# Layer 2 begins with two f pairs of one block, and x forms are written where they are read

## The chip, the cores and the metric

The kernel runs on one core of one Trainium2 chip. The metric is the device time of one execution in microseconds (us), and the figure of a kernel is the median of its runs. PE is the tensor engine, DVE the vector engine, ACT the scalar engine, POOL the GpSimd engine, SP the engine whose queue issues nearly all DMAs.

## The reference

Linear attention over 4 batches, 8 heads, 576 positions, then two feed-forward layers on the 2304 tokens that it yields. All of it is in float32.

```python
x = attn_out.transpose(0, 2, 1, 3).reshape(2304, 512)
def _moe_ref(x, w_in, w_out):      # layer 1: w_in 512 x 2048, w_out 2048 x 512
    h = x @ w_in
    return (h - np.tanh(h)) @ w_out
def _moe2_ref(x, w_in, w_out):     # layer 2, the same shapes
    h = x @ w_in
    return (h * (1.0 / (1.0 + np.exp(-1.702 * h)))) @ w_out
```

## The kernel before

**Splitting.** A float32 operand is written as a high part in float32r and a low part (operand less high part). A product then takes three matmuls (high x high, high x low, low x high). `two` (line 421) makes both parts: a copy on ACT (line 422), then a subtraction on POOL or DVE (line 423).

**Layer 1** (loop at line 720) runs in two halves of 36 steps; step numbers below count within the second half, 0 to 35. A step computes the hidden product of one f tile and one block of 512 tokens (`h_mm`, line 343), the y product of the step three back (`do_y`, line 381) and the nonlinear part (`elem1`): ACT s, w, t; DVE 370; POOL 371; DVE 372 and 373; one step later ACT 355 and POOL 357 split the result. The blocks come in the order 1, 0, 2, 4, 3; block 4 has 256 tokens and takes two f tiles per step. When a block's last y product is done, DVE adds the first half's part into it (`evac`, line 402): the y banks are free for the next block only then. Blocks 0, 1 and 2 end with the y products in steps 18, 10 and 26.

**Work of layer 2 that is done beside layer 1's second half.** From step 4 to 21, `conv_ticks` turns the int64-packed weights of the first three f pairs of layer 2 into Strassen forms: a pair has four raw blocks of 512 KB, and a tick per letter (a, b, s, c and h, d, o and e, one step each). Blocks 0 and 2 lie in a pool of two raw buffers each, 1 and 3 in `raw2`, two buffers; the results go through a ring of four `stg` tiles to DRAM (`wfi`, `wfo`). From step 20, `xprep_ticks` does the same for x of token block 0 (768 tokens; layer 2 has three such blocks): four loads `xi`, then 14 pieces, two per step. A piece makes both parts of one half of one of the seven forms P1 to P7; each of the first eight ends with a difference on DVE (line 532) that a later form needs. A form's half kt 0 has its low part on POOL, kt 1 on DVE. Each piece goes through a ring of four `xo` tiles and a store into DRAM (`xf`); after step 30 the seven forms are loaded back with the weights of pair 0.

Stores are not issued at once: `store` puts them into a list, and `flush(2)` issues those that are two steps old. SP issues its DMAs in program order, and each waits there until its data and its place are ready.

**Layer 2** (loop at line 944) goes through 24 groups (token block sb, f pair j): (0,0), (1,0), (0,1), (1,1) and so on, then block 2 with the pairs in falling order. A group has seven slots. A slot has one Strassen product (six matmuls, `h_prod`, line 816; P2 is computed one group ahead, in slot 5) and one y chunk of an earlier group (six matmuls, line 837; two in slot 3; the first stands in slot 1 of the second group). On DVE a group has sums (`h_add`, 865), products (`mul`, 880) and eight accumulations (845 for the first pair of a block, else 847). `vec` issues them after each slot, ACT and POOL split g (886, 887). The forms of block 1 are made at the start of layer 2 from slot 3 of the first group on (slot count q from 3), those of block 2 from q = 101; both at two pieces per slot. The weights of pair j lie in one of two places, by j mod 2.

```python
GROUPS = [(sb, j) for j in range(NPAIR) for sb in range(2)] + [(2, j) for j in reversed(range(NPAIR))]
SLOTS = ("P1", "P7", "P6", "P4", "P5", "P2", "P3")
...
                if 3 <= q < 98 or q > 100:
                    xticks.popleft()()
                    xticks.popleft()()
```

Of the kernel before, what the change touches and what calls it, by code (L numbers as in the profile page):

```python
# [59 lines left out]
def body(ctx, tc, qT, kT, v, om, w1, w2, out):  # L60
# [20 lines left out]
    xf = dp.tile([7, 128, 4 * TW], F32, name="xf")  # L81
# [343 lines left out]
    def conv_ticks(p, pairs, place=None):  # L425
        raw, st = {}, {}

        def load(q, k):
            if q in pairs:
                o, tag = (cv, ("raw", "ye")[k % 2]) if place or k % 2 == 0 else (p, "raw2")  # L430
                t = raw[q, k] = o.tile([128, 512, 2], I32, tag=tag, name="raw2", bufs=2)
                nc.sync.dma_start(out=t, in_=words(w2[2 * q + k % 2, :, k // 2, :]))
# [31 lines left out]
        def cho(q, k):  # L464
            if place:
                v = place(q)[1][:, k - 2]
            else:
                v = p.tile([128, 2 * 512], F32R, tag="stg", name="stg", bufs=4)
# [6 lines left out]
        def pieces(q):  # L475
# [17 lines left out]
            def out(k):  # L493
                cho(q, k)
                load(q + 1, k)
# [5 lines left out]
        def begin():  # L501
            for k in range(4):
# [4 lines left out]
    def xprep_ticks(sb, tiles, place):  # L507
# [12 lines left out]
        def tick(kt, k):  # L520
# [168 lines left out]
    wpool = {}  # L689

    def new_x2(sb, i):
        t = xform[sb, i] = wpool[sb % 2].tile([128, 2, 2, TW], F32R, tag=f"x{i}", name=f"x{i}", bufs=1)
        return t

    def load_x2(sb, i):
        nc.sync.dma_start(
            out=new_x2(sb, i).bitcast(F32), in_=xf[i].rearrange("p (k h c) -> p k h c", h=2, c=TW))
# [22 lines left out]
    for si, (key, k, fs) in enumerate(steps):  # L720
# [33 lines left out]
        if P and sp >= LAG:  # L754
            flush(2)
# [5 lines left out]
            if sp == 20:  # L761
                xload, xt = xprep_ticks(
                    0, lambda i: rp.tile([128, 2, TW], F32, tag=f"xi{i}", name="xi", bufs=1), None)
# [5 lines left out]
            if sp == 30:  # L769
                flush()  # L770
                assert not ticks and not xticks and not later
                right.close()
                wpool[0] = pool("l2right", side="right", reuse_waits="tile")
                load_x2(0, 0)
                load_win(0)
                for i in range(1, 7):
                    load_x2(0, i)
                load_wout(0)
# [154 lines left out]
    l2 = wpool[1] = pool("l2left", reuse_waits="tile")  # L933
    xload, xt = xprep_ticks(1, lambda i: ya_tile("xi"), lambda i: xform[1, i])
    xload()
    xticks.extend(xt)
# [7 lines left out]
    for n in range(NG + 1):  # L944
        sb, j = GROUPS[min(n, NG - 1)]
        for s in range(7):
# [10 lines left out]
            if n == 0 and s == 1:  # L957
                evac(*ev, 0)
                load_win(1)
                load_wout(1)  # L960
            if n == NG:
                continue
            if s == 0 and n > 2:
                at = GROUPS[n - 1]
                if at[0] == 0 and 1 <= at[1] < NPAIR - 1:
                    (load_wout if at[1] + 1 < NPRE else new_wo)(at[1] + 1)
                elif at[0] == 2 and 0 < at[1] < NPAIR - 1:
                    load_wout(at[1] - 1)
            if s == 0 and n > 1:
                if sb == 0 and 1 <= j < NPAIR - 1:  # L970
                    (load_win if j + 1 < NPRE else new_w)(j + 1)
# [80 lines left out]
```

## Time and profile before

| what | value |
|---|---|
| time, median of 3 runs (lowest to highest) | 932.94 us (932.24 to 934.09) |
| profiled execution: own time, span | 933.93 us, 932.1 us |
| mean granted clock of PE | 0.991 |
| busy: PE, PE weight loads, DVE, ACT, POOL | 906.5, 823.8, 650.5, 564.5, 465.8 us |
| share of the span: PE, PE weight loads, DVE, ACT, POOL | 97%, 88%, 70%, 61%, 50% |
| DMA | 151.83 MB, mean 163 GB/s |

The profile shows one execution. The span runs from its first to its last instruction. The granted clock is the share of full speed (2.4 GHz) that PE was given; 0.5 is 1.2 GHz. In a timeline a row is one instruction or a run of equal ones: start, duration, engine, line, what it writes and reads, and in brackets how long the engine had stood and what ended that. A DMA's landing is counted from its issue.

### The profile page before, as it was taken

The page shows a single profiled execution, that of the slowest core. Times are in us where ns is not written, and L with a number is a line of the kernel's source. Part 1 is how long each engine was busy: PE and PEld are TensorE (multiplying, and loading weights), DVE is VectorE, ACT ScalarE, POOL GpSimd, SP SyncE. Part 2 cuts the span into 40 slices and gives each one's busy share as a digit, 9 for nine tenths or more (in the row PEclk, how much of TensorE's full clock was granted, in tenths as well). Part 3 has the DMA queues.
Part 4 walks back from the last instruction along what each step waited for, and adds up shares of the span by engine and source line. Part 5 has one row for each costly group of instructions (what it writes and reads, how often), then busy time and mean ns, then how long its engine had stood idle before and what let it go on. Part 6 is the DMA issues. An engine that isn't in the chain of part 4 may idle for free.

```text
span 932.1 us, 14425 instructions
## 1 busy us (share of the span) xinstructions
PE 906.5 (97%) x5192; PEld 823.8 (88%) x5192; DVE 650.5 (70%) x1041; ACT 564.5 (61%) x1175; POOL 465.8 (50%) x361
## 2 busy tenths in 40 slices
PE   8999999999999999999979979999999998999998
PEld 6888887888899888888878869999999998999998
DVE  4899978756666655887775374488888888544444
ACT  5888878777777767877647543355555555323231
POOL 3555534546666565776746543235545565222222
PEclk9999999999999999999989998999999999999999
DMA  6787865032453322678755972115443211343532
GB/s 200 231 264 247 257 208 161 23 136 73 131 181 123 127 88 70 223 276 277 256 178 191 410 301 79 46 41 175 170 146 117 88 54 49 124 182 139 234 136 102
DMA packets 56249, 151.83 MB, mean 163 GB/s; under 512 B 6385, under 2 KB 13169, under 8 KB 53873
## 3 DMA queue, kind: packets, MB, share of 16 engines
q1 hardware_dynamic: 56032, 150.57, 47.1%
q8 instruction: 41, 0.67, 0.3%
q10 hardware_dynamic: 144, 0.33, 0.1%
q14 instruction: 32, 0.25, 0.1%
HBM read 104.48 MB, written 46.40 MB: 162 GB/s over the span
## 4 chain that ended last, share of the span: by engine, by line
PE 76%; DVE 12%; POOL 4%; issue 3%; ACT 3%; DMA 1%; SPq 0%; POOLq 0%; ACTq 0%; DVEq 0%
PE hs L837 19%; PE y L816 16%; PE y L381 16%; PE hs L343 15%; PE y L200 3%; DVE xi L532 2%; PE y L183 2%; POOL wq L371 2%; PE y L124 1%; DVE wq L373 1%; DVE raw L294 1%; PE hs L152 1%; DMA wfi<-stg 1%; POOL mq L134 1%; DVE yacc L847 1%
## 5 line engine op out<-in xcount | busy, mean ns | idle before, releaser
L837 PE MATMUL hs<-g,wout 128*128 128x384 f32 x1152 | 226.2, 335 | 0.0
L343 PE MATMUL hs<-xb,w 128*128 128x512 f32 (+1 forms) x960 | 211.1, 370 | 1.5 <-DVE t L372 1.5
L816 PE MATMUL y<-x,win 128*128 128x384 f32 x966 | 196.8, 338 | 7.8 <-ACT x L422 2.9
L837 PEld LDWEIGHTS hs<-g,wout 128*128 128x128 f32 x1152 | 203.0, 189 | 0.0
L381 PE MATMUL y<-ghi,w 128*128 128x512 f32 (+1 forms) x640 | 194.1, 371 | 5.3 <-DVE ye L402 5.2
L343 PEld LDWEIGHTS hs<-xb,w 128*128 128x128 f32 x960 | 168.5, 190 | 32.1 <-DVE t L372 1.7
L887 POOL TENSOR_TENSOR g<-sg,g 128x384 fp32r<-128x384 f32 x96 | 103.3, 1077 | 176.6 <-ACT g L886 173.9
L816 PEld LDWEIGHTS y<-x,win 128*128 128x128 f32 x966 | 170.8, 189 | 11.2 <-DVE hx L865 5.1
L357 POOL TENSOR_TENSOR glo<-wq,ghi 128x512 fp32r<-128x512 f32 x72 | 100.5, 1396 | 139.5 <-ACT ghi L355 139.5
L373 DVE COPY_PREDICATED wq<-m,t 128x512 f32<-128x512 uint16 x72 | 87.6, 1217 | 104.6 <-POOL wq L371 103.5
L847 DVE TENSOR_TENSOR yacc<-hs,yacc 128x384 f32<-128x384 f32 x168 | 92.0, 553 | 84.5 <-PE hs L837 84.5
L381 PEld LDWEIGHTS y<-ghi,w 128*128 128x128 f32 x640 | 118.0, 191 | 26.4 <-issue 6.3
L381 PE MATMUL y<-glo,w 128*128 128x512 f32 (+1 forms) x320 | 118.5, 370 | 0.0
L886 ACT CAST g<-sg 128x384 fp32r<-128x384 f32 x96 | 49.5, 516 | 92.0 <-DVE sg L880 92.0
L877 ACT ACTIVATE sg<-hx 128x384 f32<-128x384 f32 x72 | 37.9, 526 | 109.4 <-DVE hx L865 102.2
L371 POOL TENSOR_TENSOR wq<-wq,s 128x512 f32<-128x512 f32 x70 | 90.6, 1295 | 24.0 <-DVE wq L370 24.0
L134 POOL PARTITION_ALL_REDUCE mq<-pq x32 | 65.9, 2108 | 61.8 <-ACT pq L132 61.8
L363 ACT ACTIVATE s<-hs 128x512 f32<-128x512 f32 x72 | 43.0, 597 | 61.9 <-PE hs L343 61.9
L381 PEld LDWEIGHTS y<-glo,w 128*128 128x128 f32 x320 | 61.1, 191 | 9.9
L355 ACT CAST ghi<-wq 128x512 fp32r<-128x512 f32 x72 | 44.3, 616 | 29.9 <-DVE wq L373 29.9
L370 DVE SCALAR_TENSOR_TENSOR wq<-wq,hs 128x512 f32<-128x512 f32 x72 | 49.0, 681 | 17.7 <-ACT t L365 17.7
L294 DVE SCALAR_TENSOR_TENSOR raw<-raw 128x512 int32<-128x512 int32 x57 | 56.8, 996 | 1.6
(119 smaller groups left out, 1291.4 us busy)
## 6 DMA issues: line engine op xcount, KB each, us to landing
raw<-w SPq DMA_DIRECT2D x57, 512.0 KB, 4.7
xb<-xs SPq DMA_DIRECT2D x24, 512.0 KB, 5.4
win<-wfi SPq DMA_DIRECT2D x9, 1280.0 KB, 8.3
wout<-wfo SPq DMA_DIRECT2D x9, 1024.0 KB, 4.8
xf<-xo SPq DMA_DIRECT2D x14, 384.0 KB, 3.1
x<-xf SPq DMA_DIRECT2D x7, 768.0 KB, 12.5
vt<-v SPq DMA_DIRECT2D x16, 325.0 KB, 3.4
kt<-kT SPq DMA_DIRECT2D x15, 320.0 KB, 3.3
```

Of the source, the lines that this page charges most:

```text
L134: nc.gpsimd.partition_all_reduce(mqs[i, j], pq[:, j, :], channels=128, reduce_op=bass.bass_isa.ReduceOp.max)
L294: nc.vector.scalar_tensor_tensor(out=c, in0=c, scalar=3, in1=z, op0=ALU.logical_shift_left, op1=ALU.bitwise_or)
L343: nc.tensor.matmul(h[:, j * n:j * n + n], w[:, 0, a, kt * 128:kt * 128 + 128], x[:, c, kt, :n], start=(k == 0), stop=(k == 11))
L357: nc.gpsimd.tensor_tensor(out=lo, in0=g, in1=hi.bitcast(F32), op=ALU.subtract)
L371: (nc.vector if si < 2 else nc.gpsimd).tensor_tensor(out=w, in0=w, in1=s, op=ALU.mult)
L373: nc.vector.copy_predicated(out=w, mask=m.bitcast(mybir.dt.uint16), data=t)
L381: nc.tensor.matmul(y[d][:, :n], w[:, 1, a, d * 128:d * 128 + 128], g[c][:, j * n:j * n + n], start=(first and j == 0 and k == 0), stop=(la ...
L816: nc.tensor.matmul(dst, w[:, WID[name], a, kt * 128:kt * 128 + 128], xt[:, kt, c, :], start=(first and k == 0), stop=(k == 5), skip_group_ ...
L837: nc.tensor.matmul(dst, wout[j][:, f, a, d * 128:d * 128 + 128], gt[n, f, t][:, c, :], start=(k == 0), stop=(k == 5))
L847: nc.vector.tensor_tensor(out=u, in0=dst, in1=u, op=ALU.add)
L886: nc.scalar.copy(out=u[:, 0, :], in_=g)
L887: nc.gpsimd.tensor_tensor(out=u[:, 1, :], in0=g, in1=u[:, 0, :].bitcast(F32), op=ALU.subtract)
```

## The change

- `GROUPS` starts with (0,0), (0,1), (1,0), (1,1); from pair 2 on it is as before. So block 1 begins with the third group, and the weights of pairs 0 and 1 are both held until the third and fourth groups; those of pair 2 are loaded one group later.
- The seven forms of block 0 get their place in a pool of their own at the start of the second half of layer 1. The pieces are written there; the ring `xo`, the DRAM tensor `xf`, its 14 stores and 7 loads are gone. That takes room: `raw2` has one buffer for two, `stg` three for four. A pair's block 3 is loaded behind the use of its block 1 (in tick c), the next pair's block 1 behind tick e.
- The pieces for block 0 start at step 24 for step 22, at two and one per step in turn (2, 1, 2, 1, 1 in five steps). Their loads `xi` lie in the room that the weight forms have left, at step 23.
- Layer 2's pieces come one per slot. The weights of pair 1 are asked for ahead of the loads of x.
- Stores are flushed when they are one step old.

The diff, cut to its core:

```diff
-GROUPS = [(sb, j) for j in range(NPAIR) for sb in range(2)] + [(2, j) for j in reversed(range(NPAIR))]
+GROUPS = [(0, 0), (0, 1), (1, 0), (1, 1)]
+GROUPS += [(sb, j) for j in range(2, NPAIR) for sb in range(2)] + [(2, j) for j in reversed(range(NPAIR))]
+XSTEP = 23
...
-                t = raw[q, k] = o.tile([128, 512, 2], I32, tag=tag, name="raw2", bufs=2)
+                t = raw[q, k] = o.tile([128, 512, 2], I32, tag=tag, name="raw2", bufs=1 if tag == "raw2" else 2)
...
-                t = p.tile([128, 2 * 512], F32R, tag="stg", name="stg", bufs=4)[:, :512 * n]
+                t = p.tile([128, 2 * 512], F32R, tag="stg", name="stg", bufs=3)[:, :512 * n]
...
-                load(q + 1, 1)
+                load(*((q + 1, 1) if place else (q, 3)))
...
-                load(q + 1, k)
+                load(q + 1, k if place or k == 2 else 1)
...
-            v = place(i)[:, kt] if place else rp.tile([128, 2, TW], F32R, tag="xo", name="xo", bufs=4)
+            v = xform[sb, i][:, kt]
...
-            if not place:
-                store(xf[i, :, kt * 2 * TW:(kt + 1) * 2 * TW].rearrange("p (a c) -> p a c", c=TW), v.bitcast(F32))
...
         if si == per + LAG - 1:
             wst.close()
+            xpool[0] = pool("x0", side="right", reuse_waits="tile")
+            for i in range(7):
+                new_x2(0, i)
...
-            flush(2)
+            flush(1)
...
-            if sp == 20:
+            if sp == XSTEP:
+                flush()
+                assert not ticks and not later
+                right.close()
+                xr = pool("xprep", right, side="right", reuse_waits="tile")
...
-            elif xticks and sp > 21:
-                xticks.popleft()()
-                xticks.popleft()()
...
+            elif sp > XSTEP and xticks:
+                for _ in range(1 + (sp - XSTEP) % 5 % 2):
+                    xticks.popleft()()
+                if not xticks:
+                    right.close()
+                    wpool[0] = pool("w0", side="right", reuse_waits="tile")
+                    load_win(0)
+                    load_wout(0)
...
+    load_win(1)
...
             if xticks:
                 if 3 <= q < 98 or q > 100:
                     xticks.popleft()()
-                    xticks.popleft()()
-            elif n == 1 and s == 4:
+            elif n == 2 and s == 4:
```

Three places in the order of the instructions. Names: `xi` are the loaded halves of x and its differences, `xo`, `x0` to `x6` forms, `wq` and `t` of `elem1`, `ye` an evacuated block, `hx` and `sg` the sums and products of layer 2. The changed kernel's line numbers are one higher here, three lower in layer 2.

DVE, layer 1, from the predicated copy of step 22 to the evacuation of block 2 in step 26. Before, the rows of steps 24 and 25:

```order
L372 TENSOR_TENSOR t_4800<-hs_4774,t_4800 128x512
L373 COPY_PREDICATED wq_4801<-m_4802,t_4800 128x512
L532 TENSOR_TENSOR xi_4664<-xi_4665,xi_4664 128x384
L423 TENSOR_TENSOR xo_4821<-xi_4668,xo_4821 128x384
L532 TENSOR_TENSOR xi_4668<-xi_4669,xi_4668 128x384
L370 SCALAR_TENSOR_TENSOR wq_4870<-wq_4870,hs_4827 128x512
L372 TENSOR_TENSOR t_4869<-hs_4827,t_4869 128x512
L373 COPY_PREDICATED wq_4870<-m_4871,t_4869 128x512
L532 TENSOR_TENSOR xi_4664<-xi_4665,xi_4663 128x384
L423 TENSOR_TENSOR xo_4890<-xi_4668,xo_4890 128x384
L532 TENSOR_TENSOR xi_4668<-xi_4669,xi_4663 128x384
L370 SCALAR_TENSOR_TENSOR wq_4936<-wq_4936,hs_4897 128x512
```

And now, from the predicated copy of step 24 on:

```order
L374 COPY_PREDICATED wq_4867<-m_4868,t_4866 128x512
L531 TENSOR_TENSOR xi_4813<-xi_4814 128x384
L424 TENSOR_TENSOR x0_3715<-xi_4819,x0_3715 128x384
L531 TENSOR_TENSOR xi_4813<-xi_4818 128x384
L371 SCALAR_TENSOR_TENSOR wq_4929<-wq_4929,hs_4890 128x512
L373 TENSOR_TENSOR t_4928<-hs_4890,t_4928 128x512
L374 COPY_PREDICATED wq_4929<-m_4930,t_4928 128x512
L531 TENSOR_TENSOR xi_4814<-xi_4815,xi_4814 128x384
L403 TENSOR_TENSOR ye_4766<-y0_4428,ye_4766 128x512
L403 TENSOR_TENSOR ye_4766<-y1_4429,ye_4766 128x512
```

Before, three instructions on x stand behind each predicated copy from step 22 to 25, twelve in all ahead of the evacuation; now three behind that of step 24 and one behind that of step 25, and none ahead of them.

SP, layer 1, the middle pair of `conv_ticks` (its first raw loads stand further up). Before, from the load in tick s on:

```order
L432 DMA raw2_4245<-w2 128x1024
L332 DMA xb_4093<-xs_80 128x2x512
L419 DMA wfi_84<-stg_4193 128x1024
L432 DMA raw2_4295<-w2 128x1024
L394 DMA ye_4350<-yp_81 128x2x512
L419 DMA wfi_84<-stg_4292 128x512
L419 DMA wfi_84<-stg_4299 128x1024
L432 DMA raw2_4398<-w2 128x1024
L432 DMA raw2_4403<-w2 128x1024
```

And now:

```order
L433 DMA raw2_4253<-w2 128x1024
L333 DMA xb_4101<-xs_80 128x2x512
L433 DMA raw2_4302<-w2 128x1024
L420 DMA wfi_83<-stg_4299 128x512
L420 DMA wfi_83<-stg_4306 128x1024
L395 DMA ye_4359<-yp_81 128x2x512
L420 DMA wfi_83<-stg_4354 128x1024
L433 DMA raw2_4406<-w2 128x1024
L433 DMA raw2_4411<-w2 128x1024
```

The second raw load of the run was block 1 of the last pair (4295); now it is block 3 of this pair (4302), which tick d reads one step later, and block 1 of the last pair (4411) comes at the end of the run.

DVE, the start of layer 2, from the first product behind the last evacuation on. Before:

```order
L880 TENSOR_TENSOR sg_5607<-hx_5605,sg_5607 128x384
L865 TENSOR_TENSOR hx_5640<-hs_5562,s2_5629 128x384
L532 TENSOR_TENSOR xi_5587<-xi_5588 128x384
L423 TENSOR_TENSOR x0_5596<-xi_5593,x0_5596 128x384
L532 TENSOR_TENSOR xi_5587<-xi_5592 128x384
L865 TENSOR_TENSOR hx_5656<-hs_5543,s7_5609 128x384
L532 TENSOR_TENSOR xi_5588<-xi_5589,xi_5588 128x384
L423 TENSOR_TENSOR x1_5597<-xi_5592,x1_5597 128x384
L532 TENSOR_TENSOR xi_5592<-xi_5593,xi_5592 128x384
L880 TENSOR_TENSOR sg_5654<-hx_5640,sg_5654 128x384
L532 TENSOR_TENSOR xi_5588<-xi_5589,xi_5587 128x384
L423 TENSOR_TENSOR x2_5598<-xi_5592,x2_5598 128x384
```

And now:

```order
L877 TENSOR_TENSOR sg_5583<-hx_5581,sg_5583 128x384
L862 TENSOR_TENSOR hx_5611<-hs_5533,s2_5600 128x384
L531 TENSOR_TENSOR xi_5561<-xi_5562 128x384
L862 TENSOR_TENSOR hx_5624<-hs_5514,s7_5585 128x384
L424 TENSOR_TENSOR x0_5572<-xi_5567,x0_5572 128x384
L531 TENSOR_TENSOR xi_5561<-xi_5566 128x384
L877 TENSOR_TENSOR sg_5622<-hx_5611,sg_5622 128x384
L531 TENSOR_TENSOR xi_5562<-xi_5563,xi_5562 128x384
L877 TENSOR_TENSOR sg_5637<-hx_5624,sg_5637 128x384
L424 TENSOR_TENSOR x1_5573<-xi_5566,x1_5573 128x384
L531 TENSOR_TENSOR xi_5566<-xi_5567,xi_5566 128x384
L862 TENSOR_TENSOR hx_5666<-y1_5659,sp_5639 128x384
```

Before, eight of these twelve make x forms of block 1 (x0 to x2); now six do (x0 and x1), and the sums and products of the first group stand further ahead. From the product that opens the run to the sum that releases P3 of the second group (hx of s7, in slot 4 of that group) there are now 8 differences, 4 low parts, 10 sums and products and 5 copies of y chunks.

## Rows read from the trace of the kernel before

**Rows 1.** PE's waits, 470 us on: total us, times, longest us

```profile
PE y L381 <- DVE ye L402: 5.2, 1, 5.2
```

**Rows 2.** Windows: length, busy PE, PEld, DVE, ACT, POOL, clock, DMA, GB/s

```profile
480.00:490.00 10.00, 8.03 (x43) 7.57 (x44) 5.55 (x8) 0.72 (x3) 2.58 (x3) 0.73 0.68 239
...
560.00:580.00 20.00, 20.00 (x106) 20.00 (x106) 9.84 (x19) 6.74 (x16) 6.61 (x7) 0.90 0.26 93
```

**Rows 3.** Timeline of PE, layer 1: start us, duration us

```profile
432.27 0.47 PE L381 MATMUL y<-ghi,w 128*128 128x512 f32 x1
...
473.70 3.03 PE L343 MATMUL hs<-xb,w 128*128 128x256 f32 x24
...
481.97 0.55 PE L381 MATMUL y<-ghi,w 128*128 128x256 f32 x1 [5.24 <-DVE ye L402]
...
486.46 2.91 PE L343 MATMUL hs<-xb,w 128*128 128x512 f32 x12
...
489.21 0.28 PE L381 MATMUL y<-ghi,w 128*128 128x256 f32 x1
...
492.08 2.91 PE L343 MATMUL hs<-xb,w 128*128 128x512 f32 x12
```

**Rows 4.** Timeline of DVE, layer 1 and (last row) layer 2

```profile
431.44 2.48 DVE L402 TENSOR_TENSOR ye<-y,ye 128x512 f32<-128x512 f32 x4
...
478.68 0.54 DVE L532 TENSOR_TENSOR xi<-xi 128x384 f32<-128x384 f32 x1
...
479.61 1.61 DVE L532 TENSOR_TENSOR xi<-xi 128x384 f32<-128x384 f32 x1
...
481.15 2.47 DVE L402 TENSOR_TENSOR ye<-y,ye 128x512 f32<-128x512 f32 x4
...
550.77 1.36 DVE L532 TENSOR_TENSOR xi<-xi 128x384 f32<-128x384 f32 x1
```

**Rows 5.** Timeline of ACT, layer 1

```profile
408.52 0.67 ACT L283 ACTIVATE raw<-raw 128x512 f32<-128x512 f32 x1
...
414.63 0.62 ACT L355 CAST ghi<-wq 128x512 fp32r<-128x512 f32 x1 [2.17 <-DVE wq L373]
...
469.17 0.51 ACT L422 CAST xo<-xi 128x384 fp32r<-128x384 f32 x1 [0.82 <-DVE xi L532]
...
488.92 0.51 ACT L422 CAST xo<-xi 128x384 fp32r<-128x384 f32 x1 [8.87 <-DMA xf<-xo]
```

**Rows 6.** Timeline of PE, layer 2

```profile
542.28 3.51 PE L816 MATMUL hs<-x,win 128*128 128x384 f32 x18
...
557.98 2.26 PE L816 MATMUL y<-x,win 128*128 128x384 f32 x6 [2.85 <-ACT x L422]
...
568.10 1.20 PE L816 MATMUL y<-x,win 128*128 128x384 f32 x6
...
570.18 1.20 PE L816 MATMUL y<-x,win 128*128 128x384 f32 x6
...
783.59 1.31 PE L816 MATMUL y<-x,win 128*128 128x384 f32 x6 [2.60 <-DVE hx L865]
```

**Rows 7.** Timeline of SP's queue, layer 1

```profile
406.75 0.33 SPq L432 DMA_DIRECT2D raw<-w  x1
...
454.76 2.08 SPq L419 DMA_DIRECT2D wfo<-stg  x2
```

**Rows 8.** Landings: of all raw loads (L432), and of loads issued 436 to 441 us

```profile
DMA to landing us min/median/max: 3.6/5.0/12.0
...
xi<-ysf SPq DMA_DIRECT2D x4, 384.0 KB, 5.5
```

**Rows 9.** Groups of DVE, 543 to 563 us: count, busy us, mean ns

```profile
L532 DVE TENSOR_TENSOR xi<-xi 128x384 f32<-128x384 f32 x8 | 7.7, 960 | 0.0
...
L423 DVE TENSOR_TENSOR x<-xi,x 128x384 fp32r<-128x384 f32 x6 | 5.0, 829 | 0.9 <-ACT x L422 0.9
...
L880 DVE TENSOR_TENSOR sg<-hx,sg 128x384 f32<-128x384 f32 x4 | 2.2, 548 | 0.0
```

More of the change, by code (lines that the diff above doesn't have):

```diff
@@ L467, in cho @@
             else:
[L468 removed]
+                v = p.tile([128, 2 * 512], F32R, tag="stg", name="stg", bufs=3)
                 v = v.rearrange("p (h c) -> p h c", h=2)
@@ L501, in begin, with xprep_ticks @@
         def begin():
-            for k in range(4):
+            for k in range(4 if place else 3):
                 load(pairs[0], k)
         return begin, [(x, f) for q in pairs for x, f in pieces(q).items()]
-    def xprep_ticks(sb, tiles, place):
+    def xprep_ticks(sb, tiles):
         xi = {}
@@ L688, in body @@
     xform, win, wout = {}, {}, {}
-    wpool = {}
+    wpool, xpool = {}, {}
     def new_x2(sb, i):
-        t = xform[sb, i] = wpool[sb % 2].tile([128, 2, 2, TW], F32R, tag=f"x{i}", name=f"x{i}", bufs=1)
+        t = xform[sb, i] = xpool[sb % 2].tile([128, 2, 2, TW], F32R, tag=f"x{i}", name=f"x{i}", bufs=1)
         return t
-    def load_x2(sb, i):
-        nc.sync.dma_start(
-            out=new_x2(sb, i).bitcast(F32), in_=xf[i].rearrange("p (k h c) -> p k h c", h=2, c=TW))
     def new_w(j):
@@ L760, in body @@
                         ticks.popleft()[1]()
-            if sp == 20:
+            if sp == XSTEP:
[3 more added lines that the diff above has]
+                xr = pool("xprep", right, side="right", reuse_waits="tile")
                 xload, xt = xprep_ticks(
-                    0, lambda i: rp.tile([128, 2, TW], F32, tag=f"xi{i}", name="xi", bufs=1), None)
+                    0, lambda i: xr.tile([128, 2, TW], F32, tag=f"xi{i}", name="xi", bufs=1))
                 xload()
                 xticks.extend(xt)
-            elif xticks and sp > 21:
-                xticks.popleft()()
-                xticks.popleft()()
[L769 to L778, printed above, removed]
+            elif sp > XSTEP and xticks:
[6 more added lines that the diff above has]
+                    load_wout(0)
         gg = []
@@ L932, in body, with x1_tile, ssum_tile @@
     layer1.close()
-    l2 = wpool[1] = pool("l2left", reuse_waits="tile")
-    xload, xt = xprep_ticks(1, lambda i: ya_tile("xi"), lambda i: xform[1, i])
+    l2 = wpool[1] = xpool[1] = pool("l2left", reuse_waits="tile")
+    load_win(1)
+    def x1_tile(i):
+        return ssum_tile() if i == 4 else ya_tile("xi")
+    def ssum_tile():
+        return l2.tile([128, 2, TW], F32, tag="ssum", name="xi", bufs=1)
+    xload, xt = xprep_ticks(1, x1_tile)
     xload()
+    load_wout(1)
     xticks.extend(xt)
@@ L958, in body @@
                 evac(*ev, 0)
[L959 to L960 removed]
             if n == NG:
                 continue
[L963 removed]
+            if s == 0 and n > 3:
                 at = GROUPS[n - 1]
[L965 to L966 removed]
+                if n == 4:
+                    load_wout(2)
+                elif at[0] == 0 and at[1] < NPAIR - 1:
+                    new_wo(at[1] + 1)
                 elif at[0] == 2 and 0 < at[1] < NPAIR - 1:
                     load_wout(at[1] - 1)
[L969 to L971 removed]
+            if s == 0 and n > 2:
+                if n == 3:
+                    load_win(2)
+                elif sb == 0 and j < NPAIR - 1:
+                    new_w(j + 1)
                 elif sb == 2 and 0 < j < NPAIR - 1:
@@ L993, in x2_tile @@
                     if i == 4:
-                        return l2.tile([128, 2, TW], F32, tag="ssum", name="xi", bufs=1)
+                        return ssum_tile()
                     return cv.tile([128, 2, TW], F32, tag=("raw", "ye")[i % 2], name="xi", bufs=2)
-                xload, xt = xprep_ticks(2, x2_tile, lambda i: xform[2, i])
+                xload, xt = xprep_ticks(2, x2_tile)
                 xload()
```

1 line of the change is left out of this document (removed).

## The prediction

> **What bounds the kernel now.** I read the list of what the tensor engine (PE) waits for first, since PE is busy 97% of the span. From 470 us to the end its longest are 5.2 us in layer 1 behind a DVE evacuation [rows 1], 2.85 us at the start of layer 2 behind an ACT copy of a form of x, and 2.60 us at 781 us behind a DVE sum (both below). Then the windows around them: in [rows 2] the granted clock is 0.73 and 0.90 in the stretches after the first two, so PE came back at 1.2 GHz for a while. Then the timelines, to see what ended last at each place.
>
> Place A, layer 1, steps 26 and 27. PE ends the hidden product of step 27 at 476.73 (481.97 less 5.24) and stands 5.24 us [rows 3]. It then needs 486.46 - 481.97 = 4.49 us for 24 matmuls that take 492.08 - 489.21 = 2.87 us later [rows 3]: 1.62 us of half clock. Place A costs 6.86 us. What ends last: the block's last y product ended at 473.70, but DVE starts the evacuation at 481.15 [rows 4], because in four steps ahead of it DVE also made pieces of x forms, 0.54 us or 1.61 us for a difference [rows 4]. Behind that ACT stands 8.87 us for the store of a form [rows 5]; that store sits in SP's queue behind the store of the evacuated block.
>
> Place B, the start of layer 2. From 542.28 to 570.18 PE issues 102 matmuls: 18 in that row, P2, P3, P1 and P7 (24), then ten runs of six, alternately y chunks and h products. Twelve take 570.18 - 568.10 = 2.08 us in the clean stretch [rows 6], so 102 should take 17.7 us. They take 27.9, so 10.2 us are lost there, the 2.85 us wait [rows 6] and the half clock behind it included. What ends last is the row of pieces of x forms for block 1, two per slot, which DVE, ACT and POOL make while PE asks for each form almost at once.
>
> Place C, from 781 to 784 us: 2.60 us [rows 6], while the forms for block 2 are made at two pieces per slot. Elsewhere behind place B the list names no wait over 0.2 us: the rest is PE's own work.
>
> **The change, part by part.** The number of matmuls and of pieces is the same. The 14 stores of forms and 7 loads of them go. All their cost that PE sees is in place A (ACT's 8.87 us); the rest lies beside PE's work.
>
> *Place A.* DVE now has three differences and one low part ahead of the evacuation, where it had eight and four. Gone are three long differences (1.61), two short (0.54) and three low parts (about the short one's 0.54): 4.8 + 1.1 + 1.6 = 7.5 us. The evacuation moves from 481.15 to 473.6, where its input is ready at 473.70; PE needs its first tile, 0.62 us of work (2.48/4 [rows 4]), by 476.73. What could be late next is the load of x: it now uses the memory of the weight forms, so it waits for their last stores, issued by 454.76 + 2.08 = 456.8 [rows 7]. With 5.0 us for a block this size [rows 8], some 2.6 us for four issues (0.33 to 1.04 us each [rows 7]) and 5.5 us for the landing [rows 8], the last x is there at about 469.9. ACT made the same step's second piece at 469.17 before [rows 5], so it is no earlier than before and DVE's chain of one more step follows it: the evacuation's first tile is ready between 474.3 and 477. I count place A as gone, 6.9 us, and keep 1 us of it for the range.
>
> *Place B.* The second group is now of block 0, whose forms are long there, and pieces for block 1 come one per slot. What ends last is then DVE's own queue. Between the evacuation of the last block (ends one 0.62 us operation behind PE's 542.28: 542.9) and the sum that releases P3 of the second group, the new order of DVE has 8 differences, 4 low parts, 10 sums and products and 5 copies. With the means of [rows 9] (960, 829, 548 ns, the copies taken as 548) that is 7.7 + 3.3 + 5.5 + 2.7 = 19.2 us, and 0.9 us in which DVE must wait for P4. So P3 starts at 563.0 on the old time axis. PE alone would be there at 542.28 + 17.7 = 560.0; it was there at 570.18. The gain is 7.1 us and 3 us of waits remain, in three pieces of about 1 us, shorter than the two that were followed by a low clock. Bounds: with every difference and low part at 0.54 us the queue is done at 558.5 and the whole 10.2 us is gained; with all at 1.36 us (a difference in [rows 4]) it is done at 568.3 and 1.8 us is gained. Why the same shape takes either: the Trainium skill (GPSIMD Engine Reference, Specifications) says that the GpSimd engine shares its SBUF interfaces with VectorE and contends with instructions of two SBUF inputs. Our two durations of one form agree with it.
>
> *Place C.* Here too the pieces come one per slot. At two, the first eight (all with a difference) fall into four slots of 9.4 us, and DVE's work in them is 7.7 + 3.3 + 9 x 0.55 = 15.9 us: 6.6 us behind, of which PE saw 2.6, so some 4.0 us were slack. At one, they fall into eight slots of 18.7 us with 7.7 + 3.3 + 18 x 0.55 = 20.9 us of work: 2.2 us behind, within the slack. The gain is 2.6 us; bounds 0, if long differences return, and 2.6.
>
> *Piece buffers of layer 1.* The second raw buffer is gone, so the fourth block of a pair is requested only behind the third piece's use of it. In the middle pair that is at 406.75, where SP asked for another block before [rows 7]. At the median 5.0 us [rows 8] it lands at 411.75; ACT wanted it at 408.52 [rows 5]. ACT stands 3.2 us, of which 2.17 us was idle a moment later [rows 5]; 1.0 us passes on to the evacuation in step 18. That one has no margin: PE began at 432.27, DVE had made the first tile at 432.06 [rows 3, 4]. So 1.0 us is lost. Bounds from [rows 8]: at 3.6 us nothing, at 12.0 us some 8. In the first pair the following evacuation has slack, in the last pair two steps without any piece follow. The smaller ring of forms (three for four) costs nothing: flushing one step earlier issues its stores earlier by as much.
>
> *Loads of layer 2.* The third pair's weights now wait for the third group's last product, and are wanted 72 matmuls later, 12.5 us at 2.08 per twelve. Even the slowest 512 KB block of [rows 8], 12.0 us, lands in that. The second pair's weights are asked for earlier than before. Their cover is PE's own work; without it the price is the landing less 12.5 us. The forms for block 2, though slower in coming, are finished from eight slots (P2) to four (P3) ahead of their use: nothing.
>
> Sum against the profiled execution's own 933.93 us (span 932.1 and 1.8 around it): 933.93 - 6.9 - 7.1 - 2.6 + 1.0 = 918.3. That execution is 1.0 above the median of the runs, 932.94, so I say 917.3.
>
> **Rivals.**
> - *All places clean.* DVE's short durations prevail because POOL's work is spread; no loss at step 18. 932.94 - 6.9 - 10.2 - 2.6 = 913.2. For it: eight short and long differences alternate with POOL's load, which thins out. Against: POOL still makes half of the low parts.
> - *Contention at places B and C.* DVE's pieces all meet POOL and run long: 1.8 us gained at B instead of 7.1 and nothing at C, so 917.3 + 5.3 + 2.6 = 925.2. This is what the skill's sentence above would make of it if POOL never paused. In [rows 9] the mean of the differences is 0.96, midway between 0.54 and 1.36, which speaks against all being long.
> - *The x loads hold place A.* If they land 4 us later than I count, DVE's evacuation is late by about 3 us and the half clock's 1.6 us returns: 917.3 + 4.6 = 921.9. For it: they stand in SP's queue behind four stores. Against: SP has little else in these steps.
> - *Slower: one raw buffer.* ACT stands for the fourth block in each of three pairs, and the wait passes on to the evacuations. At a landing of L us PE loses L - 1.8 - 2.2 us plus 1.6 us of half clock, less the slack where there is some. Without slack three losses of 5.5 us eat the 16.6 us of gain, which is L = 7.9 us in all three pairs; at 12.0 it is 932.9 - 16.6 + 3 x 9.6 = 945.1. Against: the median is 5.0 [rows 8], and two of the three pairs have slack. The Trainium skill (Trainium Kernel Development and Optimization, Best Practices) asks for double buffering so that DMA and compute overlap, which this edit gives up. By the trace half of these blocks land within 5.0 us of being asked for, so here the rule would cost the 1.0 us of my sum, and only landings over 7.9 us make it decide.
> - *The change doesn't do what it says*: waits of equal length turn up elsewhere, 932 to 934. Against: PE's order keeps the same products, and all three causes are removed.
>
> **How the numbers follow.** Forecast (914.8 to 920.0) 0.50; all clean (912.5 to 914.8) 0.17; contention at B and C 0.13; x loads at A 0.10; no change 0.03; slower 0.07. The range that leaves out no more than 2 in 10 is 912.5 to 925.5: it takes in the clean case, contention and late x loads, and leaves out the last two cases. Faster by over 0.2% (what a measurement of this kernel can tell from no change) 0.90, within it 0.03, slower 0.07.
>
> **What would show it.** In the new profile: no wait of PE on an evacuation around step 27 and a clock of 1.00 there (place A); no ACT wait on a DMA of forms; at the start of layer 2 PE's waits are on sums of DVE (hx) alone and total about 3 us, with no stretch under clock 1.00 (place B); no wait over 1 us while the forms for block 2 are made (place C); ACT waits for DMA of raw weights, some 3 us three times, and PE waits about 1 us at step 18. Wrong it is if PE waits there for x forms, if the clock falls at the start of layer 2, or if a wait on third-pair weights appears some 60 us behind the start of layer 2.

## The result, and the profile after

The changed kernel takes 919.43 us, the median of four runs (917.95 to 921.01); the kernel before took 932.75 us beside it (932.24 to 934.09). The ratio is 0.9855 [0.9835, 0.9876]: 13.3 us faster. The prediction said 917.3, within 912.5 to 925.5. The profiled execution of the changed kernel is its quickest, 917.95 us with a span of 916.1 us. Line numbers below are those of the changed kernel.

PE's waits first, over the whole run (those of [rows 1] are from 470 us on): total us, times, longest us.

```profile
PE y L382 <- DVE ye L403: 3.2, 1, 3.2
...
PE y L813 <- DVE hx L862: 1.2, 1, 1.2
```

From 330 us on the list names no others. Where [rows 2] had a clock of 0.73 and 0.90, the same windows now show 1.00 (length, busy PE, PEld, DVE, ACT, POOL, clock, DMA, GB/s):

```profile
480.00:490.00 10.00, 10.00 (x67) 9.13 (x66) 8.26 (x12) 5.56 (x11) 4.95 (x5) 1.00 0.48 157
560.00:580.00 20.00, 20.00 (x117) 20.00 (x116) 11.19 (x23) 8.19 (x18) 7.71 (x9) 1.00 0.24 88
```

Place A and step 18 on PE and then on DVE (start, duration; in brackets how long the engine had stood, and for what):

```profile
435.08 0.47 PE L382 MATMUL y<-ghi,w 128*128 128x512 f32 x1 [3.20 <-DVE ye L403]
...
476.51 3.04 PE L344 MATMUL hs<-xb,w 128*128 128x256 f32 x24
479.38 0.28 PE L382 MATMUL y<-ghi,w 128*128 128x256 f32 x1
```

```profile
431.90 0.69 DVE L290 SCALAR_TENSOR_TENSOR raw<-raw 128x512 int32<-128x512 int32 x1 [0.96 <-ACT raw L286]
432.63 1.70 DVE L295 SCALAR_TENSOR_TENSOR raw<-raw 128x512 int32<-128x512 int32 x1
434.26 2.47 DVE L403 TENSOR_TENSOR ye<-y,ye 128x512 f32<-128x512 f32 x4
...
477.81 2.48 DVE L403 TENSOR_TENSOR ye<-y,ye 128x512 f32<-128x512 f32 x4
```

Place A, which was 5.24 us in [rows 3], is gone: the evacuation starts at 477.81, its first tile is there at 478.43 (2.48/4 later), and PE asks for it at 479.38 without a wait. A new wait stands at step 18: PE goes on at 435.08, 2.81 us later than the 432.27 of [rows 3], because DVE begins that evacuation at 434.26, where [rows 4] had 431.44. Why, ACT's and SP's timelines say (SP's rows are issues):

```profile
413.50 0.67 ACT L284 ACTIVATE raw<-raw 128x512 f32<-128x512 f32 x1 [3.79 <-DMA raw<-w]
...
430.67 0.67 ACT L284 ACTIVATE raw<-raw 128x512 f32<-128x512 f32 x1 [2.91 <-DMA raw<-w]
```

```profile
407.86 0.33 SPq L433 DMA_DIRECT2D raw<-w  x1
...
421.47 2.08 SPq L433 DMA_DIRECT2D raw<-w  x2
```

ACT stands for raw weights twice there: at 413.50 for the middle pair's block 3, asked for at 407.86, and at 430.67 for the last pair's block 1, which is the second of the two loads from 421.47 on. The second wait ends just ahead of the evacuation: DVE stands 0.96 us for ACT's piece, one of its own operations then takes 1.70 us (its neighbour, of the same shape, 0.69; POOL was at work from 432.49 to 433.78 us, see the last section), and the evacuation is queued behind it.

The start of layer 2 on PE, against [rows 6]:

```profile
537.76 3.31 PE L813 MATMUL hs<-x,win 128*128 128x384 f32 x18
...
547.69 1.34 PE L813 MATMUL y<-x,win 128*128 128x384 f32 x6 [1.20 <-DVE hx L862]
...
557.19 1.20 PE L813 MATMUL y<-x,win 128*128 128x384 f32 x6
```

The 102 matmuls of place B now take 557.19 - 537.76 = 19.43 us; before they took 27.90. Place C's wait is not in the list any more.

The account of the two profiled executions, 933.93 and 917.95 us, a difference of 15.98: place A 6.86, place B 27.90 - 19.43 = 8.47, place C 2.60, step 18 -3.20, together 14.73. The other 1.25 us is spread over stretches without a wait of its own, and I do not assign it.

### The profile page after: what moved, and what is told of

Same layout as the page of the kernel before. It is cut to its first block, busy times and chain, and to the rows that moved or that the text cites. A ratio compares the mean times of both kernels' runs of the same rounds, so it can differ in the third digit from the quotient of the medians.

```text
span 916.1 us, 14382 instructions
## 1 busy us (share of the span) xinstructions
PE 900.0 (98%) x5192; PEld 819.5 (89%) x5192; DVE 646.4 (71%) x1041; ACT 562.4 (61%) x1175; POOL 462.2 (50%) x361
## 4 chain that ended last, share of the span: by engine, by line
PE 87%; DVE 4%; ACT 2%; DMA 2%; POOL 2%; issue 2%; ACTq 0%; POOLq 0%; DVEq 0%
PE hs L834 22%; PE y L382 19%; PE hs L344 18%; PE y L813 18%; PE y L201 3%; DMA raw<-w 2%; PE y L184 2%; PE y L125 1%; PE hs L153 1%; POOL mq L135 1%; DVE pq L139 1%; POOL stg L424 1%; PE hs L813 1%; PE y L228 1%; PE y L180 1%
## 5 line engine op out<-in xcount | busy, mean ns | idle before, releaser
L813 PE MATMUL y<-x,win 128*128 128x384 f32 x966 | 194.0, 335 | 1.3 <-DVE hx L862 1.2
L358 POOL TENSOR_TENSOR glo<-wq,ghi 128x512 fp32r<-128x512 f32 x72 | 98.2, 1363 | 137.3 <-ACT ghi L356 137.3
L374 DVE COPY_PREDICATED wq<-m,t 128x512 f32<-128x512 uint16 x72 | 83.1, 1155 | 107.4 <-POOL wq L372 107.2
L295 DVE SCALAR_TENSOR_TENSOR raw<-raw 128x512 int32<-128x512 int32 x57 | 61.8, 1084 | 1.6
```

Of the source, the lines that this page charges most:

```text
L295: nc.vector.scalar_tensor_tensor(out=c, in0=c, scalar=3, in1=z, op0=ALU.logical_shift_left, op1=ALU.bitwise_or)
L358: nc.gpsimd.tensor_tensor(out=lo, in0=g, in1=hi.bitcast(F32), op=ALU.subtract)
L374: nc.vector.copy_predicated(out=w, mask=m.bitcast(mybir.dt.uint16), data=t)
L813: nc.tensor.matmul(dst, w[:, WID[name], a, kt * 128:kt * 128 + 128], xt[:, kt, c, :], start=(first and k == 0), stop=(k == 5), skip_group_ ...
```

## The experiments

Each ran beside the kernel before; us are medians, with the lowest and highest run in brackets. The kernel before had medians of 932.8, 933.4, 932.4 and 933.4 us in the four groups.

**Step 18: the raw2 buffers.** Two kernels give the second buffer back, the first with the old order of loads, the second without.

```diff
-                t = raw[q, k] = o.tile([128, 512, 2], I32, tag=tag, name="raw2", bufs=1 if tag == "raw2" else 2)
+                t = raw[q, k] = o.tile([128, 512, 2], I32, tag=tag, name="raw2", bufs=2)
...
-                load(*((q + 1, 1) if place else (q, 3)))
+                load(q + 1, 1)
...
-                load(q + 1, k if place or k == 2 else 1)
+                load(q + 1, k)
...
-            for k in range(4 if place else 3):
+            for k in range(4):
```

> The changed kernel with two raw2 buffers again and the raw loads in the order of before; all else as changed. Theory (the single raw buffer makes the 3.2 us wait of PE at the step-18 evacuation): that wait is gone, ACT's waits for raw data in the middle pair (2.5, 3.8, 2.9 us) are gone, and the time falls from 919.4 by 3.2 us and by what half clock follows that wait in some executions, so 914.5 to 916.5. Rival (the wait comes from the three stg buffers, from the earlier flush or from the x pieces): PE still stands about 3 us at step 18, 918 to 921.

Measured 914.90 (914.41 to 914.91), ratio 0.9804 [0.9791, 0.9817]. In the profile PE has one wait behind 330 us, the 1.2 us at place B, and ACT waits for no raw data between 340 and 470 us, where the changed kernel waited 14.8 us in five waits. The theory holds, and the edit is worth 4.5 us in medians. The second kernel has this line of it alone:

```diff
-                t = raw[q, k] = o.tile([128, 512, 2], I32, tag=tag, name="raw2", bufs=1 if tag == "raw2" else 2)
+                t = raw[q, k] = o.tile([128, 512, 2], I32, tag=tag, name="raw2", bufs=2)
```

> The changed kernel with two raw2 buffers and nothing else: the raw loads stay in the changed order (block 3 asked for in tick c, the next pair's block 1 behind tick e). Theory (the one buffer makes the load wait for the use of block 1): SP asks for block 3 earlier, ACT's waits for raw data and PE's 3.2 us at step 18 are gone; 914.4 to 915.5. Rival (the place of the load in SP's order is the cause, behind the weight forms' stores): PE still stands 2 to 3 us at step 18; 917 to 920.

Measured 914.79 (913.54 to 915.54), ratio 0.9813 [0.9799, 0.9827]. SP's queue, same stretch as above:

```profile
404.27 0.46 SPq L433 DMA_DIRECT2D raw<-w  x1
...
419.67 0.81 SPq L433 DMA_DIRECT2D raw<-w  x2
```

The order is that of the changed kernel. Block 3 is asked for 3.6 us earlier (404.27, not 407.86), the later two 1.8 us earlier and in 0.81 us, where they took 2.08. That is enough: ACT still waits for raw data, 3.6 us in three waits where it was 14.8 in five, but PE waits 0.7 us at most around step 18, and the medians of the two kernels are 0.1 us apart. The one buffer is the cause; the place of the loads in the queue is not.

**The ring of weight forms.** The version of the first experiment, with

```diff
-                t = p.tile([128, 2 * 512], F32R, tag="stg", name="stg", bufs=3)[:, :512 * n]
+                t = p.tile([128, 2 * 512], F32R, tag="stg", name="stg", bufs=2)[:, :512 * n]
...
-                v = p.tile([128, 2 * 512], F32R, tag="stg", name="stg", bufs=3)
+                v = p.tile([128, 2 * 512], F32R, tag="stg", name="stg", bufs=2)
```

> The version with two raw2 buffers (914.9 us) with two stg buffers in place of three. Theory (the ring of weight forms costs nothing when stores go out one step later, as I held for three against four): 914.4 to 915.4, no new wait of PE. Rival (the ring is what DVE, ACT or POOL wait for next, so its size mattered too): waits of PE on the evacuation of step 18 return, 916 to 922.

Measured 922.64 (921.92 to 923.40): the rival, 7.7 us slower than with three. ACT's waits from 400 to 470 us, and PE at step 18:

```profile
ACT stg L423 <- DMA wfo<-stg: 10.9, 2, 6.4
```

```profile
437.60 0.47 PE L382 MATMUL y<-ghi,w 128*128 128x512 f32 x1 [3.00 <-DVE ye L403]
```

With three, ACT waits for no store of a form in that stretch; with two it stands 6.4 us up to 401.72, and DVE begins the evacuation at 436.77, where it was 431.28 with three. That the one leads to the other is read from the order of the work and not shown apart. Half clock follows PE's wait here (a granted clock of 0.66 from 437 to 442 us). So one buffer less cost nothing that a wait shows, and the next one did. My reason, that stores go out one step earlier, was not tried apart from the rest.

**Place A.** Two edits of the kernel before: the pieces of steps 24 and 25 left for later, and a longer ring of stores.

```diff
-            elif xticks and sp > 21:
+            elif xticks and sp > 21 and sp not in (24, 25):
```

> The kernel before with one edit: no pieces of x in steps 24 and 25; they follow later, at the same two per step, the ring and the stores stay. Theory (place A is DVE's queue ahead of the evacuation of step 26): the 5.24 us wait near 482 us and its half clock are gone and nothing as long takes their place; the time falls from 932.8 by 5 to 7 us, to 926 to 928. Rival (the store ring of the forms, ACT's 8.87 us, holds PE): PE still stands 4 us or more there; 931 to 935.

Measured 925.22 (924.58 to 925.86), ratio 0.9915 [0.9902, 0.9929], so 6.6 to 9.1 us, the theory's 5 to 7 or somewhat more. Behind 330 us PE's waits on evacuations are, in all,

```profile
PE y L381 <- DVE ye L402: 0.5, 1, 0.5
```

The profiled executions differ by 9.35 us, but 2.75 of that is half clock at place B, whose waits are as before (last paragraph of this section). That leaves 6.6 for place A.

```diff
-            v = place(i)[:, kt] if place else rp.tile([128, 2, TW], F32R, tag="xo", name="xo", bufs=4)
+            v = place(i)[:, kt] if place else rp.tile([128, 2, TW], F32R, tag="xo", name="xo", bufs=7)
```

> The kernel before with seven xo buffers in place of four. Theory (place A is DVE's queue): ACT's wait of 8.87 us for the store of a form is gone or far shorter, PE's wait of 5.2 us at the step-26 evacuation stays within 1 us, and the time stays at 931.5 to 934. Rival (the ring of stores is the cause): PE's wait shrinks below 2 us and the time falls to 926 to 929.

Measured 932.71 (930.81 to 933.58), ratio 0.9994 [0.9985, 1.0003]. ACT waits for no store any more (its 8.87 us of [rows 5] are gone), and PE stands as before:

```profile
481.84 0.55 PE L381 MATMUL y<-ghi,w 128*128 128x256 f32 x1 [5.23 <-DVE ye L402]
```

The rival falls: place A was DVE's queue, and ACT's long wait cost nothing.

**Places B and C: the rate.** The changed kernel at two pieces per slot:

```diff
                 if 3 <= q < 98 or q > 100:
                     xticks.popleft()()
+                    xticks.popleft()()
```

> The changed kernel with layer 2's pieces at two per slot, as before; the order of the groups stays changed. Theory (the rate is what removed the wait at place C, and it serves place B too): a wait of about 2.6 us returns while the forms for block 2 are made, and PE stands 2 to 6 us more at the start of layer 2 behind sums of DVE; 923 to 929. Rival (the order of the groups alone did it, the rate does nothing): no new wait, 918 to 921.

Measured 928.20 (927.84 to 929.87): 8.8 us slower than the changed kernel. PE at places B and C:

```profile
536.14 3.31 PE L813 MATMUL hs<-x,win 128*128 128x384 f32 x18
...
542.87 1.33 PE L813 MATMUL hs<-x,win 128*128 128x384 f32 x6 [2.38 <-DVE hx L862]
...
551.73 2.10 PE L813 MATMUL y<-x,win 128*128 128x384 f32 x6 [4.21 <-DVE hx L862]
...
562.78 1.20 PE L813 MATMUL y<-x,win 128*128 128x384 f32 x6
...
775.93 1.31 PE L813 MATMUL y<-x,win 128*128 128x384 f32 x6 [2.62 <-DVE hx L862]
777.09 1.97 PE L834 MATMUL hs<-g,wout 128*128 128x384 f32 x6
```

The 102 matmuls take 562.78 - 536.14 = 26.64 us, hardly less than the 27.90 of before, and within the 25.15 to 27.93 that executions with the old order take: the new order of the groups alone gains almost nothing at B. Place C's 2.6 us returns, with half clock behind it (1.97 us for six matmuls that take 1.20 in the clean stretch).

The kernel before with block 2's pieces one per slot:

```diff
                     xticks.popleft()()
-                    xticks.popleft()()
+                    if q < 98:
+                        xticks.popleft()()
```

> The kernel before with one edit: the pieces for block 2 (slot count over 100) come one per slot, those for block 1 still two. Theory (place C alone, 2.6 us, hangs on the rate): the wait of 2.60 us near 781 us is gone and the time falls from 932.8 to about 930.2. Rival (DVE falls behind there for another reason, or the wait comes back elsewhere): 932.3 to 934.1.

Measured 928.67 (925.41 to 930.20), ratio 0.9947 [0.9931, 0.9964]. Place C is gone from the list of waits, as the theory has it, but the median fell by 4.1 us, more than its 2.6. The profiled executions also differ by 4.1 us: 2.6 is place C's wait, and 1.26 lies at place B, which this edit does not touch. There the 102 matmuls take 568.83 - 542.19 = 26.64 us behind the same waits as before, because half clock lasts shorter. So the 4.1 us are not all place C's.

The changed kernel with the group order of before and two per slot for block 1 (its weight loads go with the order):

```diff
-GROUPS = [(0, 0), (0, 1), (1, 0), (1, 1)]
-GROUPS += [(sb, j) for j in range(2, NPAIR) for sb in range(2)] + [(2, j) for j in reversed(range(NPAIR))]
+GROUPS = [(sb, j) for j in range(NPAIR) for sb in range(2)] + [(2, j) for j in reversed(range(NPAIR))]
...
                     xticks.popleft()()
+                    if q < 98:
+                        xticks.popleft()()
```

> The changed kernel with the order of the groups of before, (0,0), (1,0), (0,1), (1,1), the weight loads that go with it, and two pieces per slot for block 1; block 2 stays at one per slot, and layer 1 stays changed. Theory (the order of the groups together with the rate for block 1 is what place B is made of): PE again stands and runs at a low clock between some 540 and 570 us, and about 9 us of the gain go: 926 to 930. Rival (the start of layer 2 gained because the forms of block 0 and the weights are there earlier): 918 to 922.

Measured 925.16 (922.12 to 927.46): 5.7 us slower than the changed kernel, between the two expectations. The mechanism is the theory's: PE's longest wait in layer 2 is again 2.85 us behind ACT's copy of a form, and the 102 matmuls take 566.79 - 538.86 = 27.93 us in the profiled execution, which is the slowest of the six:

```profile
538.86 3.31 PE L812 MATMUL hs<-x,win 128*128 128x384 f32 x18
...
554.56 2.26 PE L812 MATMUL y<-x,win 128*128 128x384 f32 x6 [2.85 <-ACT x L422]
...
566.79 1.20 PE L812 MATMUL y<-x,win 128*128 128x384 f32 x6
```

Its size varies from run to run. Together with the kernel at two per slot this says that the two edits work as one: the new order leaves time to make the forms slowly, and only the slower rate uses it. The old order at one per slot was not tried: its second group would read forms of block 1 that are not yet written.

**What the remaining 1.2 us at place B is.** Four versions of the kernel of 914.90 us. First all low parts of block 1 on POOL:

```diff
-            two(v[:, 0, :], v[:, 1, :], src, (nc.gpsimd, nc.vector)[kt])
+            two(v[:, 0, :], v[:, 1, :], src, nc.vector if kt and sb != 1 else nc.gpsimd)
```

> The version with two raw2 buffers (914.9 us) with one more edit: all low parts of the forms of block 1 on POOL, none on DVE, so 1.4 us less in DVE's queue ahead of the sum that PE awaits at the start of layer 2. Theory (the remaining 1.2 us there is the length of DVE's queue): that wait is gone, 913.5 to 914. Rival (a busier POOL makes DVE's differences longer, or PE then waits for a low part of POOL): PE stands as long or longer at the start of layer 2; 914.7 to 919.

Measured 915.93 (915.51 to 916.59): 1.0 us slower, so the rival. PE stands longer, 1.55 us and not 1.21, and half clock follows in the profiled execution (a granted clock of 0.50 from 546 to 549 us):

```profile
544.91 1.61 PE L813 MATMUL y<-x,win 128*128 128x384 f32 x6 [1.55 <-DVE hx L862]
```

Then all of them on DVE:

```diff
-            two(v[:, 0, :], v[:, 1, :], src, (nc.gpsimd, nc.vector)[kt])
+            two(v[:, 0, :], v[:, 1, :], src, nc.vector if kt or sb == 1 else nc.gpsimd)
```

> The version with two raw2 buffers (914.9 us) with all low parts of the forms of block 1 on DVE, none on POOL. Theory (a DVE subtraction of two operands in memory takes 1.36 us while POOL runs and 0.55 us when it does not): DVE's differences near the start of layer 2 fall from a mean of 0.89 us to 0.6 us or less, which pays for the three or four low parts that DVE gets ahead of the awaited sum; the wait stays between 0.5 and 2 us, 914.0 to 915.5. Rival (the length of DVE's queue is its count of instructions): the wait grows by 3 to 4 times 0.9 us, to 4 or 5 us, and half clock follows; 917.5 to 920.5.

Measured 914.34 (913.37 to 915.29), as the theory has it: not slower, with more work in DVE's queue. The groups of DVE from 536 to 556 us (count, busy us, mean ns), the first kernel and then the second:

```profile
L531 DVE TENSOR_TENSOR xi<-xi 128x384 f32<-128x384 f32 x8 | 7.8, 976 | 0.0
L877 DVE TENSOR_TENSOR sg<-hx,sg 128x384 f32<-128x384 f32 x3 | 3.9, 1311 | 0.0
```

```profile
L424 DVE TENSOR_TENSOR x<-xi,x 128x384 fp32r<-128x384 f32 x10 | 6.3, 625 | 0.0
L531 DVE TENSOR_TENSOR xi<-xi 128x384 f32<-128x384 f32 x8 | 4.4, 545 | 0.0
```

With POOL's low parts gone, every difference takes 0.545 us; with all of them on POOL the mean is 0.976. Taking low parts away from DVE made the sum that PE awaits later. With all low parts on DVE, PE's waits are shorter:

```profile
539.58 1.32 PE L813 MATMUL hs<-x,win 128*128 128x384 f32 x6 [0.30 <-DVE hx L862]
...
544.67 1.31 PE L813 MATMUL y<-x,win 128*128 128x384 f32 x6 [0.65 <-DVE hx L862]
```

Then the pieces of block 1 two slots later, once alone and once with all low parts on DVE:

```diff
-                if 3 <= q < 98 or q > 100:
+                if 5 <= q < 98 or q > 100:
                     xticks.popleft()()
-            elif n == 2 and s == 4:
+            elif n == 2 and s == 5:
```

> The version with two raw2 buffers (914.9 us) with the pieces of block 1 begun two slots later (slot count from 5, not from 3). Theory (pieces ahead of the first sum that PE awaits in the second group are what delays it): two differences and a low part, some 2 us of DVE's queue, leave that place, the 1.2 us wait is gone and nothing waits for the later pieces; 913.4 to 914.0. Rival (the forms of block 1 then come late and PE waits for one of them in the third group): 914.7 to 919.

Measured 914.48 (913.76 to 914.58): 0.4 us lower, no more than the runs of a kernel differ by, and the wait stays, 1.1 us. Neither case had it right. No form comes late; but on DVE

```profile
541.31 1.19 DVE L424 TENSOR_TENSOR x<-xi,x 128x384 fp32r<-128x384 f32 x1 [1.32 <-POOL x L424]
542.43 1.36 DVE L531 TENSOR_TENSOR xi<-xi 128x384 f32<-128x384 f32 x1
543.71 0.55 DVE L862 TENSOR_TENSOR hx<-y,sp 128x384 f32<-128x384 f32 x1
```

a low part stands 1.32 us until POOL has done its own, and the sum is queued behind it and a long difference.

> The version with two raw2 buffers (914.9 us) with both edits of the start of layer 2: no low part of block 1 on POOL, and the pieces begun two slots later. Theory (contention with POOL and pieces ahead of the awaited sum are all that is left there): PE's waits of 0.6 and 0.3 us fall below 0.2 us; 913.2 to 914.2. Rival (a difference or low part that waits for its data stands in DVE's queue ahead of the sum, however few pieces are there): a wait of 0.5 to 1.2 us stays; 914.2 to 915.

Measured 913.87 (913.29 to 914.14), ratio 0.9793 [0.9779, 0.9806]: the lowest median here, though a wait of 0.6 us is left, as the rival says. DVE still stands 0.99 us for ACT's copy of the first piece ahead of the awaited sum.

**How much a wait costs beyond its own length.** No kernel was made for this; the traces of two kernels above show it. In the version with the pause in steps 24 and 25, place B has the same wait as before:

```profile
535.91 3.49 PE L816 MATMUL hs<-x,win 128*128 128x384 f32 x18
...
551.62 1.28 PE L816 MATMUL y<-x,win 128*128 128x384 f32 x6 [2.86 <-ACT x L422]
552.74 1.20 PE L837 MATMUL hs<-g,wout 128*128 128x384 f32 x6
...
561.06 1.20 PE L816 MATMUL y<-x,win 128*128 128x384 f32 x6
```

but behind it six matmuls take 1.28 us, against 2.26 in [rows 6], and the 102 take 25.15 us, against 27.90: 2.75 us less, with the same waits. The granted clock was 1.00 from 551 to 556 us here, and 0.52 from 557 to 562 us before. At place C it is the other way round in the version with the longer ring:

```profile
781.41 1.48 PE L816 MATMUL y<-x,win 128*128 128x384 f32 x6 [2.60 <-DVE hx L865]
782.68 2.12 PE L837 MATMUL hs<-g,wout 128*128 128x384 f32 x6
784.61 1.76 PE L816 MATMUL y<-x,win 128*128 128x384 f32 x6
...
788.31 1.20 PE L816 MATMUL y<-x,win 128*128 128x384 f32 x6
```

The 30 matmuls up to 788.31 take 6.90 us, for 5.20 at 2.08 per twelve; in [rows 6] the first six behind the same 2.60 us take 1.31, not 1.48, and the window from 785 to 790 us of that trace has a clock of 1.00. So a wait of 2.6 to 2.9 us at one place is followed by half clock in some executions and not in others, worth 1.7 us at C and 2.75 at B. Nor does the length of a wait decide it alone: 3.20 us at step 18 of the changed kernel is followed by a clock of 1.00 (435 to 440 us), 2.52 us at the same step in the kernel with the old group order by 0.66 (433 to 438), and the 1.55 us with all low parts on POOL by 0.50. This may be why two kernels with long waits spread far (925.4 to 930.2, 922.1 to 927.5 us), but the kernel with the pause has long waits too and lies within 1.3 us in four runs. How much of a difference of medians it makes was not shown.

## Why the prediction was right, and where not

*Place A, 6.9 us: right in mechanism and size.* It measured 6.86 us, and pausing the pieces of steps 24 and 25 alone brings 6.6. On the time axis of before, which is 2.81 us earlier here, the evacuation's first tile is ready at 475.6, within the 474.3 to 477 of the working, and 0.95 us ahead of PE. The working put ACT's 8.87 us for a store down to this place too; by the longer ring they cost nothing. The x loads were no obstacle: issued at 462.90, with a median landing of 4.3 us.

*Place B, 7.1 us: mechanism right, the term too small.* The profiled execution gained 8.5. The queue of DVE, from the end of the evacuation to that of the sum which releases P3, was taken as 19.2 us and 0.9 of waiting; it took 556.67 - 538.65 = 18.0. Three waits of PE were expected; there is one, of 1.20 us. The means of [rows 9] (0.96, 0.83 us) came from a stretch in which POOL was fed at two pieces per slot; now they are 0.89 and 0.72 us between 537 and 557 us. That DVE's durations, and not its count, decide is what the two experiments on the low parts show. The term also held up to 2.75 us of half clock that not every execution has; the experiment on the group order puts the whole of place B at 5.7 us in medians.

*Place C, 2.6 us: mechanism right, the term a lower bound.* In the execution that I read, no half clock followed; in another, of the kernel with the longer ring, it does and adds 1.7 us. The 4.1 us that undoing it gave in medians are not a measure of it, since place B varied too.

*Piece buffers, +1.0 us: the step that was mis-sized.* It cost 3.2 us in the profile, 4.5 in medians. I followed the load of block 3 (3.2 us of waiting expected, 3.79 found). PE does not wait behind that, but ticks o and e came later by it, and with them the loads that SP issues behind them: 421.47, where it is 419.67 with two buffers. I did not follow the second of these loads, the next pair's block 1, which the same edit moves: it has to wait behind tick e, and tick b of the last pair needs it in step 17, right ahead of the evacuation of step 18 with no margin. The prediction named that place for the wrong load. ACT waited five times, not three. The bounds, 0 to 8, held it. In the kernel with the old group order, which has one buffer too, half clock follows the wait at step 18; that may be the rest of the 4.5.

*Loads of layer 2, smaller ring of forms: nothing, and so it was.* No wait on weights shows in the new profile. The working compared with a block of 512 KB, but the weights come in transfers of 512, 1280 and 1024 KB; their median landings are 5.7, 8.4 and 4.8 us there, each within the 12.5 us.

*The sum.* 933.93 - 6.9 - 8.5 - 2.6 + 3.2 = 919.1 by the terms as measured, 917.95 in the profile. B came out 1.4 us better and the buffers 2.2 us worse than I said: that these errors cancelled in part was luck. The step from the profiled execution to the median had the wrong sign: the execution of before lay 1.0 us above its median, that of after 1.5 us below.

*The rivals.* Contention at B and C: the mechanism is real (last section), but at one piece per slot PE's waits were 1.2 us at B and none at C. All places clean: with the second buffer back the kernel takes 914.9 us, 1.7 above the 913.2 of that case. The slower case, one raw buffer, named the edit that did cost time, but it took a landing over 7.9 us in all three pairs for a loss, and PE waited for one evacuation only.

## What to carry over

When a buffer is taken away, list every load that has to wait for it, and follow each to the step that reads it and to what is queued behind that; the one with the least margin sets the price. Spread side work so that an engine that works in order has few pieces ahead of something that PE awaits, and look for the order of work that allows this. Moving work to an idle engine can make the busy one slower, so compare the durations on both before moving it. A wait read from one execution is a lower bound where half clock may follow.

## What the runs showed of the hardware

A DVE instruction on two 128x384 operands in memory takes 0.55 us, or up to 1.65 us, and what decides is whether POOL is at work when it begins. Rows of the version with two raw2 buffers, first DVE's and then POOL's:

```profile
543.67 0.55 DVE L531 TENSOR_TENSOR xi<-xi 128x384 f32<-128x384 f32 x1
544.14 0.54 DVE L862 TENSOR_TENSOR hx<-y,sp 128x384 f32<-128x384 f32 x1
...
545.07 1.40 DVE L531 TENSOR_TENSOR xi<-xi 128x384 f32<-128x384 f32 x1
```

```profile
543.90 1.17 POOL L884 TENSOR_TENSOR g<-sg,g 128x384 fp32r<-128x384 f32 x1 [1.04 <-ACT g L883]
545.04 1.02 POOL L424 TENSOR_TENSOR x<-xi,x 128x384 fp32r<-128x384 f32 x1
```

POOL begins in the middle of the first difference, which still takes 0.55 us. The second difference begins when POOL is at work, and ends at 546.47, 0.41 us behind the end of POOL's instruction at 546.06. From 440 to 905 us of this trace it is so throughout. All 76 subtractions and products on two memory operands that begin while POOL stands take 0.56 us or less. All 29 that take over 0.7 us began while POOL was at work, and end 0.41 to 0.42 us behind its instruction. So by these rows DVE does not work at a slower rate beside POOL: it loses most of what was left of POOL's instruction (0.85 of 0.99 us for the one above). Sums with one operand from PE's output banks do not show it: all 259 of them take 0.56 us or less, and the sum of 0.54 us above lies wholly beside POOL's split. The Trainium skill (GPSIMD Engine Reference, Specifications) says that GpSimd shares its SBUF interface with VectorE and contends with instructions of two SBUF inputs; the traces agree, and add the size. The other thing I had not expected is that the same wait at the same place (2.85 and 2.86 us, place B) is followed by 1.2 GHz in one execution and by 2.4 GHz in another, of a kernel that differs only in layer 1.
